# Attention decode with a mixer on one core: a filling unit's denominators and products at other steps, and V in loads of 16 cells ahead of a change of layer

## The chip, the cores and the metric

The kernel runs on one core of one Trainium2 chip. The metric is the device time of one execution in microseconds (us), as the median of several runs of the same program. The profile is of one further execution; its times count from the start of the span.

## What is computed

Two layers, each an attention block over a cached K and V and then a token mixer, for 2 batch rows of one token each:

```
x = x + A(layernorm(x)); x = x + B(layernorm(x)); x = x + A(layernorm(x)); x = x + B(layernorm(x))
A: q = x @ wq (32 heads of 128); scores = q.k * 128**-0.5 over 32768 cached positions;
   softmax; o = p @ v; result o @ wo.      8 heads of K and V, each for 4 heads of q
B: u = gelu(layernorm(x)^T w1 + b1), 1792 hidden; y = u w2 + b2
```

All data are float32. Both layers use the same weights and the same cache, so each layer reads the whole K and V of 2 x 8 head groups, and those reads are nearly all of the work: the arithmetic on them is small.

## The kernel before

**Units and cells.** A unit is (layer, batch row, K/V head): 2 x 2 x 8 = 32 units. A unit's K, and likewise its V, is 64 cells; a cell is a 128 x 512 float32 tile of 256 KB. One tile `mem` (line 220) holds 106 cells and takes everything that is loaded: K, V, and the weights of a head (8 cells).

**Steps.** `Order` (lines 41 to 110) writes out a list of 1024 steps by hand. A step works on 4 cells of one unit's K (`k_step`, line 328, the matmuls of line 335 into `scores`) or of its V (`v_step`, line 379, the matmuls of line 388 into `acc`); a phase of 16 steps is one unit's K or V. In the quiet parts K of a unit comes ahead of V of the unit before it. For a unit, between K and V: the maximum (`max_1`, `max_2`), the turned scores (line 365) and the exponentials on ScalarE (line 370), which leave partial sums in `lsum`. Behind V: `denominators` (line 407) adds the two sums on VectorE, sums over the partitions by a matmul (line 411) and takes the reciprocal (line 413); `take_out` (line 417) copies `acc` into a row tile; `out_1` (line 435) gathers the head's result by matmuls (line 427) and multiplies by the reciprocal (line 442); `out_2` (line 448) multiplies with `wo` into `rows` (line 451).

**The changes of layer.** Layer 1 of a batch row can start only when its layer 0 is done with attention and mixer. `Order` has two such changes, one for each batch row (`changes`, line 65): x is the last unit of the old layer, `fill` is a unit of the other batch row whose V phase runs while x's mixer is worked off, and y is the first unit of the new layer. The steps around the first change, with the numbers that the text uses: K of x (400 to 415), V of the last unit ahead of it, `before[-1]` (416 to 431), K of fill (432 to 447), V of x (448 to 463), V of fill (464 to 479), K of y (480 to 495), V of y (496 to 511). The second change has the same phases 96 steps later, with two K phases ahead of V of x. x and y share their K/V head, so the first 10 cells of K and all 64 of V that x loaded are kept in `mem` for y (`kept`).

**What hangs on which step.** `at(p, f, ...)` (line 707) makes a function run behind step p. For x, with e the last step of its V, the mixer is spread over the next steps: the layernorm at e + 2, the 14 Gelu tiles two by two with their projections from e + 3 to e + 10 (`hidden_tiles`, line 520), the copy of the rows (`take_rows`, line 463) at e + 10, and `change_0` to `change_3` (lines 565 to 594), which make y's query, at e + 11 to e + 14. For any unit whose V is not the last of its batch row and layer, `denominators` is at v_mid + 2 (two steps behind the middle of its V), `out_1` at v_end + 1 and `out_2` at v_end + 2 (lines 757 to 774). For fill, v0 = e + 1, so its denominators stood at e + 10.

**Loads and their planner.** `plan_loads` (line 113) decides, ahead of time, in which sizes and into which cells everything is loaded, and behind which step each load is issued. It goes through the steps with a clock of its own (line 34 on: 0.6024 us a cell, 1.6 us a step, and the `us` that `at` was given for the hooks), looks for each load at the sizes 32, 24, 16, 8 and 4 and at all places in `mem`, and takes the place that is free soonest. A load's step is the one behind which its cells were last read. `Order.sizes`, set by `cut` (line 97), fixes the size of chosen loads: K of y, V of fill in loads of 4 (line 93), the second half of V of x in 16, 8, 4, 4 (`TAPER`). All loads are issued by SP, in order, on one queue (line 823; weights line 816), each behind its step's semaphore and with at most 8 in flight; a load that waits holds up those behind it. The transfers of one queue are worked off in order by 16 DMA engines, each of which brings an equal part of each load.

Of the kernel before, what the change touches and what calls it, by code (L numbers as in the profile page):

```python
# [15 lines left out]
HALF = 32  # L16
# [24 lines left out]
class Order:  # L41


    def __init__(self, heads):
        far, f, s = list(range(heads - 2)), heads - 2, heads - 1
        self.steps = []
        self.pairs = []
        before = [(0, b, h) for h in far for b in (0, 1)] + [(0, 0, f)]
        x0, fill0, y0 = (0, 0, s), (0, 1, f), (1, 0, s)
        x1, fill1, y1, n = (0, 1, s), (1, 0, f), (1, 1, s), (1, 1, f)  # L50
        after = [(1, b, h) for h in far[:1:-1] for b in (0, 1)] + [(1, b, h) for b in (0, 1) for h in far[1::-1]]
        for i, u in enumerate(before):
# [12 lines left out]
        self.changes = ((x0, fill0, y0), (x1, fill1, y1))  # L65
        self.units = before + [x0, fill0, y0, x1, fill1, y1, n] + after
        self.first, self.end = {}, {}
        for p, (kind, u, g) in enumerate(self.steps):
            self.first.setdefault((kind, u), p)
            self.end[kind, u, g // HALF] = p  # L70
        byv = sorted(self.units, key=lambda u: self.first["V", u])
        self.v_before = {u: byv[i - 1] if i else None for i, u in enumerate(byv)}
        self.last_of = {
            (layer, b): max((u for u in self.units if u[:2] == (layer, b)), key=lambda u: self.end["V", u, 1])
            for layer in (0, 1)
            for b in (0, 1)
        }
        self.first_of = {
            (layer, b): min((u for u in self.units if u[:2] == (layer, b)), key=lambda u: self.end["V", u, 1])
            for layer in (0, 1)  # L80
            for b in (0, 1)
        }
        self.kept = {}
        for x, _, y in self.changes:
            for g in range(KEPT_K):
                self.kept["K", x, g] = ("K", y, g)
            for g in range(KEPT_V):
                self.kept["V", x, g] = ("V", y, g)
        self.sizes = {}
        for x, fill, y in self.changes:  # L90
            self.cut("K", y, KEPT_K, (-KEPT_K % STEP,) + (STEP,) * ((2 * HALF - KEPT_K) // STEP))
            self.cut("V", x, HALF, TAPER)
            self.cut("V", fill, 0, (STEP,) * 16)
        self.cut("V", self.last, 0, (HALF // 2, HALF // 2))
        self.cut("V", self.last, HALF, FINAL)
# [100 lines left out]
def gqa_mixer_kernel(ctx: ExitStack, tc: tile.TileContext, x, kt, v, wqo, cols, out):  # L196
# [10 lines left out]
    order = Order(HKV)  # L207
# [499 lines left out]
    def at(p, f, *args, us=0.0):  # L707
        hooks.setdefault(p, []).append((f, args))
        busy[p] = busy.get(p, 0.0) + us
# [6 lines left out]
    changed = {y: (x, fill) for x, fill, y in order.changes}  # L716
# [3 lines left out]
    for u in order.units:  # L720
# [6 lines left out]
        us = (u, mate) if b == 0 and mate not in made and (layer == 0 or h < HKV - 2) else (u,)  # L727
# [11 lines left out]
    for u in order.units:  # L739
        layer, b, h = u  # L740
        key = (layer, b)
        k_mid, k_end = end["K", u, 0], end["K", u, 1]
        v0, v_mid, v_end = first["V", u], end["V", u, 0], end["V", u, 1]
        ahead = order.v_before[u]
        p1, p2 = (k_end + 2, k_end + 4) if k_end + 4 < v0 else (k_end, k_end)
        t0 = max(k_mid, end["V", ahead, 0] if ahead else 0)
        t1 = max(k_end, end["V", ahead, 1] if ahead else 0)
        if p2 <= t0:
            at(p1, max_1, u, us=0.2), at(p2, max_2, u, us=0.2)
            at(t0, turn_scores, u, 0), at(t0, exponentials, u, 0)  # L750
        else:
            at(t0, turn_scores, u, 0)
            at(p1, max_1, u, us=0.2), at(p2, max_2, u, us=0.2)
            at(p2, exponentials, u, 0, us=5.0 if p1 == p2 else 0.0)
        at(t1, turn_scores, u, 1)
        at(max(t1, p2), exponentials, u, 1)
        at(v0 - 1 if u == order.last else v_mid + 2, denominators, u, us=0.4)
        if u == order.last:
            at(v0 - 1, take_rows, key)
            at(v0 - 1, table, AF.Gelu_apprx_tanh)  # L760
            at(v0 - 1, mix_1, key)
            at(v0 - 1, last_rows, u)
            at(v_mid, unread, u, G, 3)
            at(v_mid + 4, unread, u, P, 2)
            at(v_end - 2, take_out, u)
            at(v_end - 2, unread, u, G)
            at(v_end - 1, out_sum, u)
            at(v_end, last_mixer, u)
            continue
        at(v_end, take_out, u)  # L770
        if u != order.last_of[key]:
            late = 0 if u == order.v_before[order.last] else 1
            at(v_end + late, out_1, u, us=1.2)
            at(v_end + 2 * late, out_2, u, us=2.0)
            continue
        e = v_end
        at(e - 2, mix_1, key, us=1.2)
        at(e, out_1, u, us=1.9)
        at(e + 1, out_2, u, us=2.0)
        at(e + 1, take_rows, key)  # L780
        at(e + 2, mix_2, key, us=1.2)
        if layer == 0:
            at(e + 2, unread, u, G // 2)
            at(e + 3, half_way, key, us=1.0)
            at(e + 3, unread, u, G)
        at(e + 2, table, AF.Gelu_apprx_tanh)
# [103 lines left out]
```

## Time and profile before

| | us |
|---|---|
| median of 3 runs | 2505.46 (2503.72 to 2507.68) |
| the profiled execution | 2505.56 |
| its span, first to last instruction | 2503.7 |
| TensorE matmuls at work | 1380.4 |
| VectorE, ScalarE at work | 180.4, 185.9 |
| mean granted clock of TensorE | 0.756 of full speed |

The rows of the profile give a group of instructions or one of them: the line of the kernel, the engine (PE is TensorE, DVE VectorE, ACT ScalarE, POOL GpSimd, SP the engine that issues the loads), the operation, output and input tiles with shapes. In a timeline a row begins with start and duration in us and ends, in brackets, with the idle time of the engine ahead of it and what ended that. In the table of stretches the columns are each engine's busy time, then PEclk, the granted share of TensorE's clock, the busy share of the 16 DMA engines, and the rate in GB/s. A matmul of float32 stands as several records (8 for a step of 4 cells).

### The profile page before, as it was taken

How to read it: one execution, taken by the hardware profiler on the slowest of the kernel's cores; microseconds unless marked ns; L12 is line 12 of the kernel's file. 1: busy time of each engine (PE TensorE's matmuls, PEld its weight loads, DVE VectorE, ACT ScalarE, POOL GpSimd, SP SyncE). 2: the span in 40 equal slices, each digit the busy share in tenths (PEclk: the TensorE clock that was granted, in tenths of full speed). 3: DMA queues.
4: the chain of work that ended last, by engine and by line, in shares of the span. 5: the costliest groups of instructions: out<-in, count | busy, mean ns of one | idle time of the engine just before them, and what ended most of it. 6: DMA issues, size and time to landing. Idle time of an engine off the chain costs nothing. (4 is left out here: it accounts for less than half of the span.)

```text
span 2503.7 us, 21195 instructions
## 1 busy us (share of the span) xinstructions
PE 1380.4 (55%) x9682; PEld 395.1 (16%) x9682; DVE 180.4 (7%) x487; ACT 185.9 (7%) x579; POOL 5.2 (0%) x18
## 2 busy tenths in 40 slices
PE   3455555654555545556676773555554545555567
PEld 1111111111111111111121121111111111111112
DVE  1000000000000000001010010000000000000012
ACT  0100000000000000001110101000000000000021
POOL 0000000000000000000000000000000000000000
PEclk9777776777767776778887877777777777777788
DMA  9999999999999999999999999999999999999996
GB/s 418 431 425 436 434 431 434 434 430 432 432 434 432 430 433 434 416 430 418 407 426 427 417 424 438 432 433 429 434 434 430 434 435 428 430 436 432 432 428 278
DMA packets 33651, 1065.70 MB, mean 426 GB/s; under 512 B 3989, under 2 KB 3993, under 8 KB 5146
## 3 DMA queue, kind: packets, MB, share of 16 engines
q1 hardware_dynamic: 33272, 1064.32, 99.0%
q8 instruction: 76, 1.25, 0.2%
q14 instruction: 13, 0.11, 0.0%
q10 hardware_dynamic: 290, 0.03, 0.0%
HBM read 1064.33 MB, written 0.00 MB: 425 GB/s over the span
## 5 line engine op out<-in xcount | busy, mean ns | idle before, releaser
L388 PE MATMUL acc<-mem,S 128*16 128x512 f32 x4080 | 590.7, 711 | 575.5 <-DMA mem<-in_v_dram 570.6
L335 PE MATMUL scores<-mem,qz 128*32 128x512 f32 x4096 | 602.7, 729 | 516.8 <-DMA mem<-in_kt_dram 516.7
L370 ACT ACTIVATE S<-S,neg 128x128 f32<-128x128 f32 x256 | 129.7, 509 | 2240.4 <-DVE S L365 1201.3
L335 PEld LDWEIGHTS scores<-mem,qz 128*32 128x32 f32 x4096 | 135.9, 127 | 914.5 <-issue 470.4
L388 PEld LDWEIGHTS acc<-mem,S 128*16 128x16 f32 x4080 | 124.9, 106 | 890.1 <-issue 801.4
L345 DVE TENSOR_REDUCE mx<-scores 128x1 f32<-128x512 f32 x64 | 44.2, 691 | 803.9 <-PE scores L335 796.1
L427 PEld LDWEIGHTS misc<-selg,row 128*128 128x128 f32 x256 | 48.9, 285 | 48.2 <-issue 36.8
L427 PE MATMUL misc<-selg,row 128*128 128x4 f32 x256 | 51.7, 325 | 3.3 <-DVE row L419 3.3
L365 DVE STREAM_TRANSPOSE S<-scores 128x512 f32<-128x512 f32 x64 | 45.5, 710 | 111.6 <-PE acc L388 111.6
L451 PE MATMUL rows<-mem,oT 128*1 128x512 f32 x248 | 52.5, 936 | 0.3 <-DVE oT L442 0.3
L370 ACT ACTIVATION_READ_ACCUMULATOR S<-S,neg 128x1 f32 x256 | 47.7, 186 | 0.0
L355 DVE TENSOR_REDUCE m<-misc 1x4 f32<-1x128 f32 x32 | 8.9, 279 | 379.0 <-PE misc L353 379.0
L419 DVE COPY row<-acc 128x512 f32<-128x512 f32 x32 | 22.1, 692 | 176.1 <-PE acc L388 176.1
L413 DVE RECIPROCAL rl<-misc 128x4 f32<-128x4 f32 x32 | 5.8, 183 | 360.9 <-PE misc L411 360.9
L442 DVE TENSOR_TENSOR oT<-misc,rl 128x4 f32<-128x4 f32 x32 | 5.2, 162 | 273.1 <-PE misc L427 272.6
L411 PEld LDWEIGHTS misc<-both,one 128*128 128x128 f32 x64 | 14.4, 280 | 52.7 <-issue 46.8
L300 PE MATMUL misc<-mem,xw 128*32 128x512 f32 x144 | 20.0, 618 | 1.9 <-DVE xw L276 1.9
L353 PE MATMUL misc<-ident,mxa 128*1 128x128 f32 x64 | 18.5, 387 | 2.1 <-DVE mxa L351 2.1
L307 PEld LDWEIGHTS misc<-selg,row 128*128 128x128 f32 x128 | 16.3, 199 | 17.1 <-issue 8.6
L411 PE MATMUL misc<-both,one 128*128 128x4 f32 x64 | 17.1, 338 | 3.2 <-DVE both L410 3.2
L527 ACT ACTIVATE row<-bcast,bias,scale 128x512 f32<-128x512 f32 x21 | 16.3, 778 | 31.2 <-PE rows L511 14.2
L307 PE MATMUL misc<-selg,row 128*128 128x2 f32 (+1 forms) x128 | 17.7, 260 | 0.8 <-DVE row L292 0.8
(119 smaller groups left out, 245.6 us busy)
## 6 DMA issues: line engine op xcount, KB each, us to landing
mem<-in_kt_dram SPq DMA_DIRECT2D x20, 2048.0 KB, 16.1
mem<-in_v_dram SPq DMA_DIRECT2D x37, 1024.0 KB, 8.8
mem<-in_wqo_dram SPq DMA_DIRECT2D x14, 2048.0 KB, 32.0
mem<-in_kt_dram SPq DMA_DIRECT2D x28, 1024.0 KB, 9.1
mem<-in_v_dram SPq DMA_DIRECT2D x7, 4096.0 KB, 23.6
mem<-in_v_dram SPq DMA_DIRECT2D x4, 6144.0 KB, 26.3
mem<-in_kt_dram SPq DMA_DIRECT2D x6, 4096.0 KB, 23.8
mem<-in_v_dram SPq DMA_DIRECT2D x7, 2048.0 KB, 27.1
```

Source lines behind the costliest of these rows:

```text
L300: nc.tensor.matmul(q_ps[us][32 * d : 32 * d + 32, :], xw[:, d, :], wq[:, d, :], start=True, stop=True)
L307: nc.tensor.matmul(pt[:, r * n : (r + 1) * n], q_row[us][:, r * DH : (r + 1) * DH], side, start=True, stop=True,)
L335: nc.tensor.matmul(sc_ps[u, half][32 * row : 32 * row + 32, :], qz[:, at : at + 32], cells(at_cell["K", u, g], 1), start=(i == 0), stop=(i ...
L345: nc.vector.tensor_reduce(mx[u][:, half : half + 1], sc_ps[u, half], axis=AX.X, op=ALU.max)
L353: nc.tensor.matmul(pm[:1, :P], mxa, ident, start=True, stop=True)
L365: nc.vector.transpose(S[half], sc_ps[u, half])
L370: nc.scalar.activation(s[:, :, h], s[:, :, h], AF.Exp, bias=neg[u][:, h : h + 1], scale=SCALE, accum_out=lsum[u][:, half, h : h + 1],)
L388: nc.tensor.matmul(acc[32 * row : 32 * row + R * QT, :], S[half][:, col : col + R * QT], vc, start=(g < NG), stop=(g >= quads - NG),)
L411: nc.tensor.matmul(pl[:, :R], ones, both, start=True, stop=True)
L419: nc.vector.tensor_copy(asb[u], acc)
L427: nc.tensor.matmul(po_of[u][:, :R], asb[u][:, t * DH : (t + 1) * DH], selg[:, t * R : (t + 1) * R], start=(t == 0), stop=(t == QT - 1 and ...
L451: nc.tensor.matmul(rows[b][32 * r : 32 * r + 1, :], oT[u][:, r : r + 1], wo_of(u)[:, r, :], start=(u == order.first_of[layer, b]), stop=(u ...
```

## The change

Three edits. `Order` now also fixes V of the last unit ahead of the first change as four loads of 16 cells, and the first half of V of each x as two loads of 16. For the filling units, `denominators` moves from v_mid + 2 to v0 + 4, that is from e + 10 to e + 5, behind the third pair of Gelu tiles; and `out_1` and `out_2` move from v_end + 1 and v_end + 2 to v_end + 7 and v_end + 9, that is from behind y's first and second K steps to behind its seventh and ninth. The planner runs again on the new sizes and hook times, so the places and steps of other loads follow from it.

```
@@ class Order
         self.sizes = {}
+        self.cut("V", before[-1], 0, (HALF // 2,) * 4)
         for x, fill, y in self.changes:
+            self.cut("V", x, 0, (HALF // 2, HALF // 2))
             self.cut("K", y, KEPT_K, (-KEPT_K % STEP,) + (STEP,) * ((2 * HALF - KEPT_K) // STEP))
             self.cut("V", x, HALF, TAPER)
             self.cut("V", fill, 0, (STEP,) * 16)
@@ hooks of each unit
         at(t1, turn_scores, u, 1)
         at(max(t1, p2), exponentials, u, 1)
-        at(v0 - 1 if u == order.last else v_mid + 2, denominators, u, us=0.4)
+        fills = [y for y, (_, fill) in changed.items() if fill == u]
+        at(v0 - 1 if u == order.last else v0 + 4 if fills else v_mid + 2, denominators, u, us=0.4)
@@
         at(v_end, take_out, u)
         if u != order.last_of[key]:
-            late = 0 if u == order.v_before[order.last] else 1
+            late = 0 if u == order.v_before[order.last] else 7 if fills else 1
             at(v_end + late, out_1, u, us=1.2)
-            at(v_end + 2 * late, out_2, u, us=2.0)
+            at(v_end + (late + 2 if fills else 2 * late), out_2, u, us=2.0)
             continue
```

More of the change, by code (lines that the diff above doesn't have):

```diff
@@ L89, in __init__ @@
         self.sizes = {}
+        self.cut("V", before[-1], 0, (HALF // 2,) * 4)
         for x, fill, y in self.changes:
+            self.cut("V", x, 0, (HALF // 2, HALF // 2))
             self.cut("K", y, KEPT_K, (-KEPT_K % STEP,) + (STEP,) * ((2 * HALF - KEPT_K) // STEP))
@@ L756, in gqa_mixer_kernel @@
         at(max(t1, p2), exponentials, u, 1)
-        at(v0 - 1 if u == order.last else v_mid + 2, denominators, u, us=0.4)
+        fills = [y for y, (_, fill) in changed.items() if fill == u]
+        at(v0 - 1 if u == order.last else v0 + 4 if fills else v_mid + 2, denominators, u, us=0.4)
         if u == order.last:
@@ L771, in gqa_mixer_kernel @@
         if u != order.last_of[key]:
-            late = 0 if u == order.v_before[order.last] else 1
+            late = 0 if u == order.v_before[order.last] else 7 if fills else 1
             at(v_end + late, out_1, u, us=1.2)
-            at(v_end + 2 * late, out_2, u, us=2.0)
+            at(v_end + (late + 2 if fills else 2 * late), out_2, u, us=2.0)
             continue
```

## The prediction

> **What bounds the kernel now.** Three views, from coarse to fine. First the page: which engine is ever full?
>
> ```profile
> span 2503.7 us, 21195 instructions
> PE 1380.4 (55%) x9682; PEld 395.1 (16%) x9682; DVE 180.4 (7%) x487; ACT 185.9 (7%) x579; POOL 5.2 (0%) x18
> q1 hardware_dynamic: 33272, 1064.32, 99.0%
> q8 instruction: 76, 1.25, 0.2%
> L388 PE MATMUL acc<-mem,S 128*16 128x512 f32 x4080 | 590.7, 711 | 575.5 <-DMA mem<-in_v_dram 570.6
> L335 PE MATMUL scores<-mem,qz 128*32 128x512 f32 x4096 | 602.7, 729 | 516.8 <-DMA mem<-in_kt_dram 516.7
> ```
>
> No compute engine passes 55%, and nearly all the idle time of TensorE's two big lines ends on a DMA. Queue q1 is at work for 99% of the span. So the time is 1064.32 MB divided by the rate of the transfers, and a change that moves no bytes can win only what that rate loses somewhere. Second view: the rate by stretches, quiet ones first and last, the stretches around the two changes of layer between them.
>
> ```profile
> core 0: us, PE busy (x) PEld busy (x) DVE busy (x) ACT busy (x) POOL busy (x), PEclk, DMA share, GB/s
> 500.00:1000.00 500.00, 255.82 (x1736) 72.00 (x1732) 29.71 (x77) 25.32 (x96) 0.00 (x0) 0.72 1.00 432
> 1040.00:1100.00 60.00, 28.20 (x198) 7.13 (x198) 2.23 (x7) 2.11 (x8) 0.00 (x0) 0.72 0.98 415
> 1100.00:1150.00 50.00, 20.02 (x152) 5.99 (x144) 3.01 (x6) 2.11 (x8) 0.00 (x0) 0.70 0.97 418
> 1150.00:1230.00 80.00, 61.26 (x468) 19.56 (x472) 9.00 (x33) 17.95 (x35) 1.09 (x2) 0.93 1.01 423
> 1230.00:1270.00 40.00, 29.33 (x186) 5.54 (x182) 3.57 (x9) 4.14 (x16) 0.00 (x0) 0.71 1.00 402
> 1360.00:1435.00 75.00, 57.99 (x432) 16.86 (x428) 9.11 (x31) 15.88 (x27) 1.08 (x2) 0.90 1.01 419
> 1435.00:1475.00 40.00, 33.26 (x246) 9.02 (x242) 3.87 (x11) 4.14 (x16) 0.00 (x0) 0.79 0.99 412
> 1600.00:2400.00 800.00, 420.24 (x2868) 119.05 (x2870) 49.67 (x131) 47.09 (x167) 0.54 (x1) 0.73 1.00 432
> ```
>
> Quiet stretches run at 432 GB/s. Against that, a stretch loses its length times (1 - rate/432): 2.4 us in 1040-1100, 1.6 in 1100-1150, 1.7 in 1150-1230, 2.8 in 1230-1270, 2.3 in 1360-1435, 1.9 in 1435-1475. That is 12.7 us, half a per cent, and it is the ceiling. The two V stretches of the filling units (1150-1230 and 1360-1435) are transfers of 4 cells without a pause (share 1.01); the load lists that the planner's code gives for both kernels hold 65 loads of 4 cells each, so those 4.0 us stay. 8.7 us are left.
>
> Third view, the landings. A load counts as landed when the slowest of the 16 DMA engines has brought its part, and that is what TensorE waits for. Its own starts show it, in the K phase of the first new unit y:
>
> ```profile
> 1229.54 1.93 PE L335 MATMUL scores<-mem,qz 128*32 128x512 f32 x8 [1.43 <-DMA mem<-in_kt_dram]
> 1232.02 1.93 PE L335 MATMUL scores<-mem,qz 128*32 128x512 f32 x8 [0.55 <-DMA mem<-in_kt_dram]
> 1234.50 1.67 PE L335 MATMUL scores<-mem,qz 128*32 128x512 f32 x8 [0.55 <-DMA mem<-in_kt_dram]
> 1236.97 1.06 PE L335 MATMUL scores<-mem,qz 128*32 128x512 f32 x8 [0.80 <-DMA mem<-in_kt_dram]
> 1239.43 1.93 PE L335 MATMUL scores<-mem,qz 128*32 128x512 f32 x8 [1.40 <-DMA mem<-in_kt_dram]
> 1242.19 1.93 PE L335 MATMUL scores<-mem,qz 128*32 128x512 f32 x8 [0.83 <-DMA mem<-in_kt_dram]
> ...
> 1247.11 1.06 PE L335 MATMUL scores<-mem,qz 128*32 128x512 f32 x8 [0.75 <-DMA mem<-in_kt_dram]
> ```
>
> Each row is one step of 4 cells that starts as its load lands. The landings stand 2.46 to 2.48 us apart (the two gaps up to 1247.11 too); one gap, 1239.43 to 1242.19, is 2.76. So where the window says 2.8 us lost, the landings say 0.3. The same in the second change:
>
> ```profile
> 1439.75 1.93 PE L335 MATMUL scores<-mem,qz 128*32 128x512 f32 x8 [0.55 <-DMA mem<-in_kt_dram]
> 1442.69 1.93 PE L335 MATMUL scores<-mem,qz 128*32 128x512 f32 x8 [1.00 <-DMA mem<-in_kt_dram]
> ```
>
> One gap of 2.94, so 0.5 lost. The windows average over 16 engines, most of which were ahead and paused; the landings follow the slowest, and the end of the program waits for the slowest too. I weigh the landings more.
>
> **The change part by part.** The working starts from the profiled execution's 2505.56 us (span 2503.7 and 1.86 around it); the median of the runs, 2505.46, is 0.1 less.
>
> (a) V ahead of the first change in loads of 16. Before, V of the last unit ahead of the change came as 16+16+24+8 cells, K of the filling unit as 32+24+8, V of x as 24+8+16+8+4+4. After: 16+16+16+16, then 32+32, then 16+16+16+8+4+4. The first two loads wait for the same steps in both lists, so the thin place around 1060 stays. What follows differs (TensorE's timeline, with SP's row last):
>
> ```profile
> 1075.92 5.01 PE L388 MATMUL acc<-mem,S 128*16 128x512 f32 x32 [5.50 <-DMA mem<-in_v_dram]
> 1090.55 3.61 PE L388 MATMUL acc<-mem,S 128*16 128x512 f32 x16 [9.62 <-DMA mem<-in_v_dram]
> 1116.04 1.94 PE L335 MATMUL scores<-mem,qz 128*32 128x512 f32 x8 [15.51 <-DMA mem<-in_kt_dram]
> 1130.59 7.07 PE L335 MATMUL scores<-mem,qz 128*32 128x512 f32 x64 [2.13 <-DMA mem<-in_kt_dram]
> 1092.51 0.33 SPq L823 DMA_DIRECT2D mem<-in_kt_dram  x1
> ```
>
> Between 1090.55 and 1116.04 40 cells landed (8 of V, 32 of K), 10.49 MB, 24.3 us at 432 GB/s; it took 25.5. So at most 1.2 us are lost, at a load that SP could send only at 1092.51, since it waited for the step fed by the 24-cell load. After, the load of 16 and K's 32 both wait for step 423, the last of the four that start at 1075.92, so they go out near 1081, with 16 cells (9.7 us from 1075.9, to 1085.6) still on their way. No late load is left. From 1116.04 to 1130.59 24 cells took 14.55 us, the full rate, so nothing more is there to win. This part is worth between 0 and -1.2; a fetch of instructions (q8 is in the table above) can hold up one engine just as well, and I take a third, **-0.4**.
>
> (b) The list that follows. The planner places each load in the 106 cells by its own clock, so new sizes and due times shift all later places. For y's K, with steps counted from y's first, each load of 4 cells (named by its first cell) goes out behind this step:
>
> ```
> cell     24  28  32  36  40  44  48  52  56  60
> before    0   1   3   4   5   5   8   9  10  12
> after     1   3   4   5   7   7   8  10  10  12
> ```
>
> Both changes have these two rows. Before, SP sent nothing for 7.5 us (its timeline, then the time to landing of its loads from 1215 to 1245):
>
> ```profile
> 1225.68 0.80 SPq L823 DMA_DIRECT2D mem<-in_kt_dram  x2
> 1234.02 0.33 SPq L823 DMA_DIRECT2D mem<-in_kt_dram  x1
> 1244.19 1.28 SPq L823 DMA_DIRECT2D mem<-in_kt_dram  x3
> DMA to landing us min/median/max: 5.4/10.3/13.3
> ```
>
> The fastest load took 5.4 us from issue to landing, of which 2.5 are the transfer. So **a load is late on the slowest engine when less than 2.9 us of transfers are queued ahead of it**. Before, the load behind step 8 (1234.02) had three ahead, the last landing at 1239.4: 5.4 us, plenty. The one behind step 12 (1244.19) had two, the last landing at 1247.1: 2.9, just enough. After, step 7 starts at 1229.54 and is done 1.93 later; cells 40 and 44 go out at 1231.5 with cells 32 and 36 ahead, the last landing at 1234.5: 3.0. Step 10 starts at 1236.97 and is done 1.06 to 1.93 later, with two ahead to 1241.9 (2.48 behind 1239.43): 3.0 to 3.9. Step 12 again 2.9 to 3.9. So there are two or three thin places where there was one, all at the edge. Cost: if both pauses go with the old gaps, -0.8 by the landings and -4.7 by the windows; if each change pauses twice as often as it does now, +0.8 and +4.7. I stay near the landings' end and take **+0.5**. The Trainium skill ("DMA: Bandwidth & Descriptors", Anatomy of one DMA) puts the fixed part of a transfer at about 2.0 us, fitted on another issuing path; the 5.4 above leaves 2.9, so here the trace decides. By 2.0 every thin place has 0.9 to spare, +0.5 becomes 0, and the sum 2505.2.
>
> (c) The filling unit's denominators, from the last Gelu step to the third.
>
> ```profile
> 1201.04 0.69 DVE L465 COPY row<-rows 128x512 f32<-128x512 f32 x1 [15.46 <-PE rows L511]
> 1201.95 0.35 PE L411 MATMUL misc<-both,one 128*128 128x4 f32 x2 [1.04 <-DVE both L410]
> 1202.23 1.05 PE L388 MATMUL acc<-mem,S 128*16 128x512 f32 x8
> ```
>
> VectorE makes the sum `both` behind its copy of the rows, so TensorE's matmul stood 1.04 us for it, until 1201.95, and the V step behind it began 0.3 us late. Moved, the add and the reciprocal fall into VectorE's idle 15.46 us ahead of that copy, and the 0.35 of matmul among Gelu projections. TensorE's V steps here take 1.05 us (last row) and their loads of 4 cells land 2.5 us apart, so over a microsecond of each is free and covers 0.35 either way: between -0.3 and +0.4 per change by the rows, **0** taken, as no landing moves. If the cover went, it would be +0.7 for both changes.
>
> (d) The products, 7 and 9 steps behind V's end instead of 1 and 2.
>
> ```profile
> 1216.26 1.06 PE L427 MATMUL misc<-selg,row 128*128 128x4 f32 x8
> 1218.13 1.04 PE L451 MATMUL rows<-mem,oT 128*1 128x512 f32 x8
> 1222.22 1.07 PE L335 MATMUL scores<-mem,qz 128*32 128x512 f32 x8 [1.33 <-DMA mem<-in_kt_dram]
> ```
>
> 2.1 us of TensorE leave steps 0 to 3 of y's K, which run ahead of their data only until 1222.22. The 1.06 goes between steps 6 and 7, where TensorE stood 1.43 us (row 1229.54): hidden. The 1.04 goes behind step 8, whose own load is sent by then; the wait there is 0.55, so step 9 begins 0.5 late, but no load of the new list waits for step 9, and step 10 begins at its landing. VectorE's copy and product are early in both. Bounds: -2.1 to +2.1 per change, **0** taken. The Trainium skill ("TensorE: Matmul & The Clock Gate", Part 1) says that idling halves TensorE's clock and some microseconds of work restore it; the 1.93 and 1.06 for the same 8 matmuls agree. By it, products among these steps keep step 7 at 1.06, its loads leave 0.9 us sooner, +0.5 becomes 0, and the sum is again 2505.2.
>
> **Sum:** 2505.56 - 0.4 + 0.5 + 0 + 0 = **2505.7 us**. No DMA is added (230 loads for 231), none changes its queue, and bytes and the other instructions are the same in number.
>
> **Rivals.** *Faster, the pauses go:* the windows are right, not the landings. Then (b) gives -4.7 and (a) up to -1.6 (1100-1150): 2499.3. For it: 402 and 412 GB/s are real. Against it: the landings lost 0.8, and the new list keeps thin places. 5 in 100.
>
> *Slower, the ring runs dry:* two or three places at the edge become late loads, since step 7 and step 10 both run at the slow 1.93. It decides when queued work falls under 2.9 us, so from a TensorE delay of 0.1 us at step 7. Price: the pauses' windows again for each of them, 4.7 for a second one, up to 9.4 for a third; with (a) not gained, 2510.3 to 2515.0, 2511 as its value. For it: 3.0 against 2.9. Against it: before had 2.9 at 1244.19, and the next landings, to 1247.1, were not late. 10 in 100.
>
> *Slower by the products:* TensorE gets behind at steps 7 and 9 for want of cover, 2.1 us in each change straight into landings: +4.2, 2509.8, still within 0.2%. 4 in 100.
>
> *Nothing moves:* the cuts shift loads that nobody waits for, 2505.6. This can't be told from the forecast and shares its chance, 81 in 100.
>
> **How the numbers follow.** 0.2% is 5.0 us, about what a measurement of this kernel can tell from no change. Faster by more: the first rival, 0.05. Slower by more: the second, about 0.09 of its 0.10. Within: 0.86. The single terms' far ends are -6.3 and +9.4; they hold each other off, so the forecast's own range is 2503 to 2508.5, and with half of the two larger rivals 2501.5 to 2510.5.
>
> **What would show it.** In the changed kernel's trace: (a) SP sends two loads near 1081 and none near 1092, and 25.5 us becomes about 24.3; (b) loads of y's K leave at about 1231.5, 1234 and 1238, and gaps of landings stay under 2.9 us; more than two gaps above 3 per change mean the second rival; (c) no wait of L411 on VectorE at 1201; (d) L427 just ahead of 1229.5 and L451 near 1234, with L335's waits on DMA between them. Wrong I am if 1230-1270 and 1435-1475 come to 425 GB/s or more (the first rival) or fall under 385.

## The result, and the profile after

The changed kernel takes **2508.44 us** (median of 20 runs, 2505.84 to 2516.12) beside 2505.38 for the kernel before on the same chip (20 runs, 2502.66 to 2510.19). The ratio is 1.0015, with a 95% interval of 1.0008 to 1.0021: 3.1 us or 0.15% slower, small but clear of zero. The forecast was 2505.7, its range 2501.5 to 2510.5. So the direction and the bounds held, and the size of the loss did not: 3.1 measured, 0.1 to 0.2 forecast (2505.7 beside the profiled execution's 2505.56 and the median of 2505.46). The direction owes something to luck: it was what was left of two close estimates, -0.4 and +0.5.

The first view is the page of the changed kernel. The lines are those shown of the kernel before, two line numbers higher in the code (L337 is K's matmul, L390 V's).

```profile
span 2507.4 us, 21193 instructions
PE 1396.2 (56%) x9682; PEld 398.8 (16%) x9682; DVE 180.5 (7%) x487; ACT 185.8 (7%) x579; POOL 5.2 (0%) x18
q1 hardware_dynamic: 33128, 1064.32, 98.9%
L390 PE MATMUL acc<-mem,S 128*16 128x512 f32 x4080 | 596.7, 719 | 553.8 <-DMA mem<-in_v_dram 548.9
L337 PE MATMUL scores<-mem,qz 128*32 128x512 f32 x4096 | 609.9, 738 | 527.8 <-DMA mem<-in_kt_dram 527.4
```

The same bytes, the same number of matmuls, TensorE still idle for its loads. The page cannot say where 3 us went; the table of stretches can, at least roughly.

```profile
core 0: us, PE busy (x) PEld busy (x) DVE busy (x) ACT busy (x) POOL busy (x), PEclk, DMA share, GB/s
1040.00:1100.00 60.00, 30.69 (x190) 7.39 (x194) 2.23 (x7) 2.11 (x8) 0.00 (x0) 0.70 0.98 413
1100.00:1150.00 50.00, 27.80 (x196) 7.95 (x184) 3.46 (x8) 2.11 (x8) 0.00 (x0) 0.75 0.99 425
1150.00:1230.00 80.00, 57.90 (x428) 17.37 (x428) 8.57 (x31) 17.98 (x35) 1.09 (x2) 0.90 1.01 420
1230.00:1270.00 40.00, 28.74 (x202) 6.27 (x202) 3.57 (x9) 4.14 (x16) 0.00 (x0) 0.77 0.99 400
1360.00:1435.00 75.00, 57.92 (x432) 18.09 (x424) 9.12 (x31) 15.88 (x27) 1.08 (x2) 0.91 1.00 411
1435.00:1475.00 40.00, 31.04 (x226) 8.55 (x230) 3.87 (x11) 4.14 (x16) 0.00 (x0) 0.78 0.97 402
```

1100-1150 rose from 418 to 425 GB/s. The second change fell: 1360-1435 from 419 to 411, 1435-1475 from 412 to 402. TensorE's timeline of y's K in the second change shows the places. A row with x8 is one step of 4 cells, x16 two; the last row is y's first V.

```profile
1416.53 1.06 PE L337 MATMUL scores<-mem,qz 128*32 128x512 f32 x8 [1.41 <-DMA mem<-in_kt_dram]
1419.01 1.93 PE L337 MATMUL scores<-mem,qz 128*32 128x512 f32 x8 [1.42 <-DMA mem<-in_kt_dram]
1420.87 1.87 PE L429 MATMUL misc<-selg,row 128*128 128x4 f32 x8
1422.67 3.39 PE L337 MATMUL scores<-mem,qz 128*32 128x512 f32 x16
1425.89 1.03 PE L453 MATMUL rows<-mem,oT 128*1 128x512 f32 x8
1426.75 1.03 PE L337 MATMUL scores<-mem,qz 128*32 128x512 f32 x8
1430.12 1.07 PE L337 MATMUL scores<-mem,qz 128*32 128x512 f32 x8 [2.34 <-DMA mem<-in_kt_dram]
...
1440.70 1.07 PE L337 MATMUL scores<-mem,qz 128*32 128x512 f32 x8 [1.07 <-DMA mem<-in_kt_dram]
1444.96 1.94 PE L337 MATMUL scores<-mem,qz 128*32 128x512 f32 x8 [3.19 <-DMA mem<-in_kt_dram]
...
1451.84 2.76 PE L390 MATMUL acc<-mem,S 128*16 128x512 f32 x12 [2.40 <-ACT S L372]
```

Count the steps from the end: 1444.96 is step 15, 1430.12 step 10, 1416.53 step 5. Two steps stand far behind their forerunners, step 10 by 3.37 us and step 15 by 4.26, and both wait for a DMA. From the start of step 5 to that of step 15 are ten loads of 4 cells, 24.8 us at their undisturbed distance of 2.48. Here it took 28.43; before it took 25.27 (1417.42 to 1442.69). This one number, **step 5 to step 15**, is the measure of most experiments below, since it looks only at the place and not at what a run lost earlier.

Why is step 10's load late? It, with step 11's, was sent here (SP's timeline; first the changed kernel, then the kernel before):

```profile
1424.67 0.91 SPq L826 DMA_DIRECT2D mem<-in_kt_dram  x2
```

```profile
1418.55 0.81 SPq L823 DMA_DIRECT2D mem<-in_kt_dram  x2
```

Six microseconds later, and behind step 7 instead of step 5, as the table in the prediction said. In the trace the last load ahead of it landed at 1426.37: 1.7 us of transfers were left in the queue, and the new load landed at 1430.07, 5.4 us after it was sent. (A load has landed when the last of the 16 DMA engines has brought its part; the trace has the time of each part, and times of landing that stand in no row are from there.)

Step 15's load was sent here:

```profile
1437.38 0.33 SPq L826 DMA_DIRECT2D mem<-in_kt_dram  x1
```

The load ahead of it landed at 1440.66, so 3.3 us were queued, more than the 2.9 that the prediction asked for. It still landed 4.26 us behind that one, at 1444.92.

### The profile page after: what moved, and what is told of

Its sections match the earlier page's. It is cut to its first block, busy times and chain, and to the rows that moved or that the text cites. A ratio compares the mean times of both kernels' runs of the same rounds, so it can differ in the third digit from the quotient of the medians.

```text
span 2507.4 us, 21193 instructions
## 1 busy us (share of the span) xinstructions
PE 1396.2 (56%) x9682; PEld 398.8 (16%) x9682; DVE 180.5 (7%) x487; ACT 185.8 (7%) x579; POOL 5.2 (0%) x18
## 5 line engine op out<-in xcount | busy, mean ns | idle before, releaser
L390 PE MATMUL acc<-mem,S 128*16 128x512 f32 x4080 | 596.7, 719 | 553.8 <-DMA mem<-in_v_dram 548.9
L337 PE MATMUL scores<-mem,qz 128*32 128x512 f32 x4096 | 609.9, 738 | 527.8 <-DMA mem<-in_kt_dram 527.4
L337 PEld LDWEIGHTS scores<-mem,qz 128*32 128x32 f32 x4096 | 138.0, 129 | 933.3 <-issue 487.4
L390 PEld LDWEIGHTS acc<-mem,S 128*16 128x16 f32 x4080 | 125.8, 107 | 876.1 <-issue 775.0
L429 PEld LDWEIGHTS misc<-selg,row 128*128 128x128 f32 x256 | 49.7, 289 | 48.9 <-issue 39.3
L429 PE MATMUL misc<-selg,row 128*128 128x4 f32 x256 | 52.5, 328 | 3.3 <-DVE row L421 3.3
L413 PEld LDWEIGHTS misc<-both,one 128*128 128x128 f32 x64 | 13.5, 264 | 50.3 <-issue 45.7
L413 PE MATMUL misc<-both,one 128*128 128x4 f32 x64 | 16.4, 326 | 2.0 <-DVE both L412 2.0
```

The lines of the kernel that those rows point to most:

```text
L337: nc.tensor.matmul(sc_ps[u, half][32 * row : 32 * row + 32, :], qz[:, at : at + 32], cells(at_cell["K", u, g], 1), start=(i == 0), stop=(i ...
L390: nc.tensor.matmul(acc[32 * row : 32 * row + R * QT, :], S[half][:, col : col + R * QT], vc, start=(g < NG), stop=(g >= quads - NG),)
L413: nc.tensor.matmul(pl[:, :R], ones, both, start=True, stop=True)
L429: nc.tensor.matmul(po_of[u][:, :R], asb[u][:, t * DH : (t + 1) * DH], selg[:, t * R : (t + 1) * R], start=(t == 0), stop=(t == QT - 1 and ...
```

## The experiments

Each was timed in five rounds against the kernel before on the same chip. Beside them the kernel before took 2505.66 us (runs 1 to 4), 2505.45 (5 to 8), 2505.48 (9 to 11) and 2506.73 (12). The theory at the start: the loss comes from y's K loads, which the new list sends later. The rivals: the loads of 16, the denominators, or the products holding TensorE at steps 7 and 9.

**1. The change without the late products** (edit against the changed kernel):

```
-            late = 0 if u == order.v_before[order.last] else 7 if fills else 1
+            late = 0 if u == order.v_before[order.last] else 1
-            at(v_end + (late + 2 if fills else 2 * late), out_2, u, us=2.0)
+            at(v_end + 2 * late, out_2, u, us=2.0)
```

> The changed kernel with the products back behind y's first and second K steps; the V loads of 16 and the early denominators stay. The planner then gives y's K the old list (nothing behind step 7). Theory 1, the new list of y's K loads costs the 3 us: they are gone, about 2505.0, since the late load of 1092 is gone too. Theory 2, the products themselves cost by holding TensorE at steps 7 and 9: the same, 2505.0. Theory 3, the loads of 16 ahead of the first change cost: 2508.4 stays. V of the second y begins about 1449 by theories 1 and 2, about 1452 by theory 3 (1449.6 before, 1451.8 in the changed kernel).

Measured: 2504.61, ratio 0.9998 (0.9989 to 1.0006). Steps 5 to 15 took 24.83 us in the first change and 24.81 in the second. The loss is gone, with the loads of 16 and the early denominators still in. What also went: without the late products the planner gives y's K the places in `mem` that it had before.

**2. The late products alone** (the kernel before with the last edit of the change and nothing else).

> The kernel before with only the products moved to 7 and 9 steps behind V's end. The planner gives y's K a list that sends two loads behind step 7, as in the changed kernel. Theories 1 and 2: about 3 to 3.5 us over before, 2508.5 to 2509, with a gap of landings of over 3 us behind step 9 of the second y. Theory 3: no difference from before, 2505.4.

Measured: 2515.38, ratio 1.0036 (1.0022 to 1.0049; 5 runs). The planner made a third list, of 239 loads. For the ten loads of y's K from cell 24 on, its first change has the steps and places of the changed kernel's list; its second has the same steps from cell 40 on, and six other places. Steps 5 to 15 took 27.03 and 25.79 us, 2.5 more than before in all (25.04 and 25.27), and the stretch 1230-1270 fell to 388 GB/s. That is half of the 5.2 us by which this profiled execution (2510.87) was slower, and a quarter of the median's 9.7; the rest lies elsewhere in that list and stays open.

**3. The whole change with the old list**: the products run late, but the planner is told of them at the old steps.

```
-    def at(p, f, *args, us=0.0):
+    def at(p, f, *args, us=0.0, plan=None):
-        busy[p] = busy.get(p, 0.0) + us
+        plan = p if plan is None else plan
+        busy[plan] = busy.get(plan, 0.0) + us
...
+            late_1, late_2 = (7, 9) if fills else (late, 2 * late)
+            plan_1, plan_2 = (1, 2) if fills else (late, 2 * late)
+            at(v_end + late_1, out_1, u, us=1.2, plan=v_end + plan_1)
+            at(v_end + late_2, out_2, u, us=2.0, plan=v_end + plan_2)
```

> All of the change in what the engines do, products at 7 and 9 included, but the planner is told that the products are at 1 and 2, so that y's K keeps the old list. Theory 1 (the list): 2505.0. Theory 2 (the products hold TensorE): step 7 still begins late, but no load hangs on it in this list, and the load behind step 8 has 5 us queued: 2505.0 to 2506. Theory 3 (loads of 16): 2508.4. A result near 2508 with a late step 7 would say that the products cost by another way than the loads.

Measured: 2504.44, ratio 0.9996 (0.9987 to 1.0005); steps 5 to 15 in 24.84 and 24.82 us. In its second change TensorE was held by the products just as in the changed kernel:

```profile
1421.13 1.87 PE L429 MATMUL misc<-selg,row 128*128 128x4 f32 x8
1422.93 3.41 PE L337 MATMUL scores<-mem,qz 128*32 128x512 f32 x16
1426.16 1.03 PE L453 MATMUL rows<-mem,oT 128*1 128x512 f32 x8
1427.02 1.03 PE L337 MATMUL scores<-mem,qz 128*32 128x512 f32 x8
1429.18 1.06 PE L337 MATMUL scores<-mem,qz 128*32 128x512 f32 x8 [1.13 <-DMA mem<-in_kt_dram]
```

Step 10 begins at 1429.18, on the beat, because its load had been sent earlier. So with this list the late products cost nothing that shows in the time. The list decides.

**4. The new list alone**: as in 3, but `late_1, late_2 = (1, 2)` and `plan_1, plan_2 = (7, 9)`.

> The other cross: the planner is told that the products are at 7 and 9 and gives the changed kernel's list of loads to the letter, but the products run behind y's first and second K steps as before. Theory 1 (the list alone): 2508.4, the loads behind step 7 are late with no help of the products. Theory 2 (the products): step 7 begins as its data land and its loads leave about 1.2 us sooner in the second change, with 3 us queued: 2505.0 to 2506, and no gap of landings over 3 us at y's cells 40 to 43.

Measured: 2507.49, ratio 1.0008 (0.9999 to 1.0017): by the interval just short of clear. The profile is plainer: 26.84 and 27.11 us from step 5 to step 15, and in the second change this gap, with TensorE free of the products (TensorE's rows of steps 8 to 10):

```profile
1425.53 1.67 PE L337 MATMUL scores<-mem,qz 128*32 128x512 f32 x8 [0.56 <-DMA mem<-in_kt_dram]
1427.97 1.06 PE L337 MATMUL scores<-mem,qz 128*32 128x512 f32 x8 [0.76 <-DMA mem<-in_kt_dram]
1432.27 1.93 PE L337 MATMUL scores<-mem,qz 128*32 128x512 f32 x8 [3.24 <-DMA mem<-in_kt_dram]
```

Step 10's load, with step 11's, is this row of SP's timeline:

```profile
1425.03 0.81 SPq L829 DMA_DIRECT2D mem<-in_kt_dram  x2
```

The load left at 1425.03, with transfers queued until step 9's landing at 1427.97: 2.9 us, which the prediction called just enough. The next landing came 4.30 later, not 2.48.

**5. The denominators alone** (the kernel before with the second edit of the change).

> The kernel before with only the denominators moved among the Gelu tiles; every load is the same, behind the same step. Theory 1 (the list of y's K loads costs): no difference, 2505.5 within 1 us, since landings set the pace there and TensorE had over a microsecond of idle time a step. A rival: the earlier denominators free TensorE ahead of y's query and win about 1 us, which would be what the kernels with the old list show.

Measured: 2504.92, ratio 0.9998 (0.9989 to 1.0007); 24.79 us in both changes. Nothing to see, as forecast.

**6. The changed kernel's list with the products at steps 6 and 9** (`late_1, late_2 = (6, 9)`, `plan_1, plan_2 = (7, 9)`), so that they no longer stand ahead of step 7.

> The changed kernel with its list of loads to the letter, but the first products one step earlier, 6 steps behind V's end, ahead of a step that no load waits for. Step 7 then begins as its data land, also where the clock is low. Theory 1 (the list alone): about 2507.5, as with the list and early products, since 2.9 us of queued transfers are too few by themselves. Theory 2 (the products hold step 7): about 2505.5. The changed kernel itself has 2508.4.

Measured: 2508.99, ratio 1.0015 (1.0006 to 1.0023), no better than the change. Its profiled execution, though, was the fastest of the eleven, at 2505.36 us: 24.83 and 26.39 us. With the new list the loss differs from one execution to the next.

**7. Two loads put behind a later step** (the kernel before; the steps of cells 40 and 44 overwritten in the finished list, their places left):

```
+    held = {("K", y, g) for y in changed for g in (40, 44)}
+    loads = [(l, n, c, first["K", l[1]] + 7 if l in held else p) for l, n, c, p in loads]
```

> The kernel before with one thing changed: of y's K, the loads of cells 40 and 44 are held back from step 5 to step 7, in both changes of layer; places, sizes, order and all hooks stay. Theory 1: this alone brings most of the loss, 2 to 3 us over before, 2507.5 to 2508.5, with a gap of landings of over 3 us ahead of cells 40 in one or both changes. If it does not (under 1 us over before), the list costs by its other places: the steps of cells 24, 28 and 52, or the loads behind y's V.

Measured: 2505.53, ratio 0.9997 (0.9988 to 1.0006); 24.83 and 25.38 us. At first this looked like the end of the theory. Run 9 showed what it was worth.

**8. A try at something faster**: run 1 with the second half of K of x in two loads of 16 as well.

```
+            self.cut("K", x, HALF, (HALF // 2, HALF // 2))
```

> A version to beat both: loads of 16 and early denominators as in the change, products back behind y's first and second K steps (the old list of y's K loads), and also the second half of K of x in two loads of 16 instead of one of 32, so that V of the last unit ahead of the change need not wait until 1062 for its second load. If the pause there costs its full window (about 2 to 3 us): 2502 to 2503. If, as the landings say, it costs little because the slowest engine never paused: 2504 to 2504.5, like the kernel without the late products.

Measured: 2505.18, ratio 1.0003 (0.9994 to 1.0012). The stretch 1040-1100 stayed at 416 GB/s (415 before). No gain.

**9, 10, 11. Whole rows put behind later steps.** In the kernel before, the steps in the list were overwritten for all of y's K (run 9), for its cells 24 to 36 (run 10), and for the K that follows it (run 11). Run 9:

```
+    row = {24: 1, 28: 3, 32: 4, 36: 5, 40: 7, 44: 7, 52: 10}
+    held = {("K", y, g): first["K", y] + k for y in changed for g, k in row.items()}
+    loads = [(l, n, c, held.get(l, p)) for l, n, c, p in loads]
```

> The kernel before, with the same loads in the same cells, and with all of y's K held to the new list's steps: the loads of cells 24, 28, 32 and 36 go out behind steps 1, 3, 4 and 5 (before: 0, 1, 3 and 4), those of cells 40 and 44 behind step 7, that of cell 52 behind step 10. Nothing else of the change is in it. Theory (the steps of y's K in the new list cost the time): from 2505.5 to about 2508.5, 1230-1270 at 395 GB/s or less, 1435-1475 at 410 or less, a landing gap of more than 3.5 us in the second change. Rival (the row is covered by what is queued, and the loss comes with other cells and with the K loads that follow): 2505 to 2506, both windows at 415 or more.

> The kernel before, with only the loads of y's cells 24, 28, 32 and 36 held one step later (behind steps 1, 3, 4 and 5), so that one load of 1 MB fewer is in flight in steps 0 to 5. If the queue's depth there is what the new list costs: 2507 to 2508.5, with 1230-1270 or 1435-1475 under 410. If the depth there is more than enough: 2505 to 2506. If it is only both together with the two loads behind step 7 (held alone they cost nothing), this stays at 2505.5 and the kernel with the whole row goes up.

> The kernel before, with y's K as it was and only the loads behind it held as in the new list: in the first change the next unit's K from cell 22 on goes out behind steps 499, 500, 504 and 510 (before: 497, 497, 501 and 507), in the second one load behind step 594 (before: 593). Theory (y's own row costs the time): 2505.5, no difference. Rival (the loads that follow y's K cost it): 2507.5 to 2508.5, with 1270-1360 or 1475-1600 lower by 5 GB/s or more.

Measured: 2503.74 (0.9999, 0.9990 to 1.0008), 2503.26 (0.9994, 0.9985 to 1.0003) and 2505.40 (1.0004, 0.9995 to 1.0013): no difference in any. But the edits had not done what they were written for. In run 9 step 10's load should have waited for step 7. SP's row of it, then TensorE's rows of steps 5 to 7:

```profile
1417.05 0.80 SPq L826 DMA_DIRECT2D mem<-in_kt_dram  x2
```

```profile
1415.92 1.07 PE L335 MATMUL scores<-mem,qz 128*32 128x512 f32 x8 [1.28 <-DMA mem<-in_kt_dram]
1418.41 1.94 PE L335 MATMUL scores<-mem,qz 128*32 128x512 f32 x8 [1.42 <-DMA mem<-in_kt_dram]
1420.89 1.93 PE L335 MATMUL scores<-mem,qz 128*32 128x512 f32 x8 [0.55 <-DMA mem<-in_kt_dram]
```

It left at 1417.05, as step 5 ended (1415.92 + 1.07), and before step 7 had begun. The section on the kernel before says that each load goes out behind its step's semaphore; these runs show it more exactly. A step in the list only sets a load's place in the program; SP runs ahead, and what a load truly waits for is the last reader of the cells that it overwrites (this one goes into 94 to 97, which steps 4 and 5 read). Run 7's left at 1416.37 in the same way, and in all four runs the loads that were to be held left as the same steps ended as in the kernel before. So runs 7, 9, 10 and 11 said nothing on the theory, for or against. They show instead that the *places* have to be changed, and, as they move their loads at the same steps as the kernel before, how far such kernels scatter: ratios of 0.9994 to 1.0004.

**12. The new places alone.** The kernel before, same sizes, same order, products early; only y's K goes to the places of the new list, in both changes (cell of K above, cell of `mem` below):

```
cell of y's K   24   28   32   36   40   44   48   52   56   60
before          24   28  102   98   94   90  102   98   94  102
after           28  102   98   94  102   90   98  102   94   98
```

```
+    cell = {24: (28, 1), 28: (102, 3), 32: (98, 4), 36: (94, 5), 40: (102, 7)}
+    cell.update({44: (90, 7), 48: (98, 8), 52: (102, 10), 56: (94, 10), 60: (98, 12)})
+    moved = {("K", y, g): (c, first["K", y] + k) for y in changed for g, (c, k) in cell.items()}
+    moved["K", (0, 1, 7), 10] = (94, 495)
+    loads = [(l, n, *moved.get(l, (c, p))) for l, n, c, p in loads]
```

The new row leaves cells 24 to 27 of `mem` empty, so the places behind them move up by one. Seven of the ten loads then wait for a reader one or two steps further on, those of cells 40 and 44 for step 7 instead of step 5; the loads of cells 48, 56 and 60 wait for the same step as before.

> The kernel before, with the same loads, sizes and order, the products early and no V loads of 16; only the cells of SBUF into which the last ten loads of y's K go are those of the new list in both changes (28, 102, 98, 94, 102, 90, 98, 102, 94, 98 in place of 24, 28, 102, 98, 94, 90, 102, 98, 94, 102), and in the first change one K load behind them goes one step later, because it shares cells with y's last one. This is asked because in the kernels whose loads were only put behind later steps (the two loads, the first four, the whole row, the next K) SP sent them at the same times as before (cells 40 and 44 of the second change 1417.05 us in the kernel with the whole row, 1418.55 in the kernel before): what times a load is the last reader of the cells that it goes into, and those kernels left the cells alone. Theory (the new cells are read later, so the loads leave later and the queue runs thin): cells 40 and 44 of the second change leave SP about 1424 to 1425, as in the changed kernel and in the one with only its list, one or two landing gaps over 3.5 us in a change, second V of y at 1450 or later, time 2507 to 2509. Rival (what costs is in the rest of the list): loads leave later but land without a gap, 2505 to 2506.

Measured: steps 5 to 15 took 25.58 and **28.32 us** (28.43 in the changed kernel). SP's rows of step 10's and step 13's loads, then TensorE's rows of steps 9 to 13:

```profile
1423.82 0.80 SPq L828 DMA_DIRECT2D mem<-in_kt_dram  x2
1432.46 0.80 SPq L828 DMA_DIRECT2D mem<-in_kt_dram  x2
```

```profile
1427.07 1.06 PE L335 MATMUL scores<-mem,qz 128*32 128x512 f32 x8 [1.14 <-DMA mem<-in_kt_dram]
1430.47 1.94 PE L335 MATMUL scores<-mem,qz 128*32 128x512 f32 x8 [2.34 <-DMA mem<-in_kt_dram]
1432.95 1.94 PE L335 MATMUL scores<-mem,qz 128*32 128x512 f32 x8 [0.54 <-DMA mem<-in_kt_dram]
1435.41 1.93 PE L335 MATMUL scores<-mem,qz 128*32 128x512 f32 x8 [0.53 <-DMA mem<-in_kt_dram]
1439.89 1.93 PE L335 MATMUL scores<-mem,qz 128*32 128x512 f32 x8 [2.55 <-DMA mem<-in_kt_dram]
```

The loads left when the theory said (1423.82 for "about 1424 to 1425"), and the gaps came: 3.40 at step 10, 4.48 at step 13. The time was 2507.55, ratio 1.0005 (0.9996 to 1.0015): inside the 2507 to 2509 expected, but only 0.8 us over its own kernel before (2506.73), and the interval takes in the change's 1.0015 as well as no loss. So the time does not settle whether y's places make up all of the loss. It is the profile that carries this run, together with the table of all of them (one profiled execution each):

| y's K in | kernel | steps 5 to 15, first + second change, us | median us |
|---|---|---|---|
| old places | before | 25.04 + 25.27 | 2505.38 |
| | 1, 3, 5, 8 | 24.83 + 24.81, 24.84 + 24.82, 24.79 + 24.79, 24.84 + 24.84 | 2504.61, 2504.44, 2504.92, 2505.18 |
| | 7, 9, 10, 11 | 24.83 + 25.38, 25.93 + 25.01, 24.83 + 24.81, 24.84 + 24.83 | 2505.53, 2503.74, 2503.26, 2505.40 |
| later places | change | 26.21 + 28.43 | 2508.44 |
| | 2, 4, 6, 12 | 27.03 + 25.79, 26.84 + 27.11, 24.83 + 26.39, 25.58 + 28.32 | 2515.38, 2507.49, 2508.99, 2507.55 |

The sums of the old places lie between 49.58 and 50.94, mean 49.93; those of the later places between 51.22 and 54.64, mean 53.31. No kernel crosses over, in the profile or in the ratio of times (0.9994 to 1.0004 and 1.0005 to 1.0036), though the two ratios at the border lie close together. The difference of the means is **3.4 us**.

Does the depth of the queue make the late loads, as the theory says? For each of the ten loads of y's K from cell 24 on, in both changes of all 14 kernels, the traces give how much was queued when it was sent (until the landing of the load ahead) and how far its landing came behind that one, beyond 2.48 us (one profiled execution each; the border of 4.0 us was drawn with the numbers at hand):

| y's K in | queued, us | loads | over 0.5 us late | late in all, us |
|---|---|---|---|---|
| old places | 4.0 or more | 162 | 1 | 1.3 |
| | under 4.0 | 18 | 1 | 1.6 |
| later places | 4.0 or more | 74 | 0 | 2.6 |
| | under 4.0 | 26 | 11 | 16.0 |

So it does: 16.0 of the 18.6 us that the five kernels with the later places lost come with their 26 thinly covered loads, two or three in each change; the old places have one in each change. Also at like depth the later places were late more often (11 of 26 beside 1 of 18), and why is not shown.

No version beat the kernel before: the lowest of those that keep the change's other edits, run 3 at 2504.44, has an interval that takes in no difference.

## Why the prediction was right, and where it was not

**(a) V in loads of 16: -0.4, about right, for another reason.** The two loads were to leave near 1081 with none at 1092 (SP's timeline, the changed kernel):

```profile
1082.04 0.33 SPq L826 DMA_DIRECT2D mem<-in_v_dram  x1
1082.41 0.42 SPq L826 DMA_DIRECT2D mem<-in_kt_dram  x1
```

They did, and SP sent nothing more until 1102.15. V's last 16 cells start at 1095.57 and K's first step at 1114.93:

```profile
1095.57 6.50 PE L390 MATMUL acc<-mem,S 128*16 128x512 f32 x32 [3.26 <-DMA mem<-in_v_dram]
1114.93 1.94 PE L337 MATMUL scores<-mem,qz 128*32 128x512 f32 x8 [12.85 <-DMA mem<-in_kt_dram]
```

The 32 cells between them took 19.36 us, where 432 GB/s gives 19.42: no loss is left there. But the load sent late, at 1092.51, had not lost anything before either. In the kernel before, its 32 cells landed 19.38 us behind V's last 8 (1096.62 to 1116.00). Those 8 cells, sent at 1070.19, are what came late: 6.21 us behind the load ahead, where 432 GB/s gives 4.85. Fifteen engines had brought their part by 1095.29, the last at 1096.62; a fetch of instructions of 1.04 us began at 1094.07. That fits the fetch which the prediction named beside its own cause; which engine the fetch was on, the trace does not tell.

Over all kernels the size came out. From the landing of V's second load of 16 cells to that of K's first load (64 cells, 38.8 us at 432 GB/s) the eight kernels with the old loads there took 38.8 to 40.8 us, mean 39.5 (the kernel before 40.1), and the six with loads of 16 took 39.0 to 39.4, mean 39.2. That is 0.3 less, within the scatter. The times can't show it: of the runs that keep this part and not the new places, 1 and 3 have ratios of 0.9998 and 0.9996, and 8 has 1.0003, none clear of 1.

**(b) y's K loads: the step that failed.** The sign was right, and so was the table of steps behind which the loads go out. The loads of cells 40, 48 and 52 left at 1230.21, 1232.70 and 1236.94 in the first change, each 1.1 to 1.3 us ahead of the forecast since the whole phase had begun earlier. The thin places were there, and the gaps did not stay under 2.9 us, as the forecast had it; but there were at most two over 3 us in a change, so by the prediction's own test it was not yet the rival in which the ring runs dry. What was wrong is the price: +0.5 forecast, **+3.4** by the measure above. In the medians, beside their own kernel before, the change stands 3.1 us higher and runs 4, 6 and 12 stand 1.8, 3.5 and 0.8.

The price rested on a threshold: a load is late when under 2.9 us are queued ahead, and places at 2.9 to 3.9 cost next to nothing. The runs bear out neither half. The 5.4 us at 1244.19, from which it was taken, do not measure what a load needs: 2.9 us were queued ahead of that load and its transfer takes 2.48, so it could not land sooner. In the first change of run 6, step 10's load left with 2.5 us queued (the load ahead landed at 1233.13) and was on the beat all the same; it landed at 1235.62, 2.49 us behind. SP's row, then TensorE's row of step 10:

```profile
1230.63 0.80 SPq L829 DMA_DIRECT2D mem<-in_kt_dram  x2
```

```profile
1235.66 1.06 PE L337 MATMUL scores<-mem,qz 128*32 128x512 f32 x8 [1.32 <-DMA mem<-in_kt_dram]
```

And places on the safe side were late: 2.9 us queued cost 1.8 us in run 4 (4.30 for 2.48) and 2.0 in run 12 (4.48); 3.9 and 3.3 cost 1.1 and 1.8 in the two changes of the changed kernel. At 1.7 queued the loss was 1.2 there, just 2.9 less 1.7, but 1.5 and 0.6 in run 2. So a place under 4 us is a draw, between nothing and 2 us. By the table of depths the later places have some five of them in a kernel, late by 0.6 us on average: about 3 us.

The Trainium skill ("DMA: Bandwidth & Descriptors", Anatomy of one DMA) gives a fixed part of about 2.0 us, for another issuing path. The trace agrees for most of the engines in one thinly covered load: of that sent at 1424.67, fifteen of the 16 had brought their part 4.2 to 4.5 us later, which is 1.7 to 2.0 more than the 2.48 of the transfer. The last one took 5.4, and it is the last one that TensorE waits for.

The prediction also named a wrong cause for the new list. It put it down to new sizes and due times together. Run 1 has the new sizes and the old row; run 3 differs from the changed kernel, and run 1 from run 4, only in the steps at which the products' 1.2 and 2.0 us are booked with the planner, and the loss goes with the booking. The edit that costs is thus the third one, not by its matmuls but by what it tells `plan_loads`.

**(c) The denominators: 0, held.** Run 5 shows no difference. In the changed kernel no L413 is left at the copy of the rows near 1201, and V's next step waits for its load alone:

```profile
1201.25 0.69 DVE L467 COPY row<-rows 128x512 f32<-128x512 f32 x1 [11.99 <-PE rows L513]
1202.10 1.05 PE L390 MATMUL acc<-mem,S 128*16 128x512 f32 x8 [0.99 <-DMA mem<-in_v_dram]
```

**(d) The products: 0, held for the whole, not for the place.** In the first change they lie as forecast:

```profile
1225.73 1.07 PE L337 MATMUL scores<-mem,qz 128*32 128x512 f32 x8 [1.41 <-DMA mem<-in_kt_dram]
1226.72 1.05 PE L429 MATMUL misc<-selg,row 128*128 128x4 f32 x8
1228.22 1.93 PE L337 MATMUL scores<-mem,qz 128*32 128x512 f32 x8 [0.44 <-DMA mem<-in_kt_dram]
1230.71 1.94 PE L337 MATMUL scores<-mem,qz 128*32 128x512 f32 x8 [0.56 <-DMA mem<-in_kt_dram]
1232.42 1.93 PE L453 MATMUL rows<-mem,oT 128*1 128x512 f32 x8
```

Step 7 at 1228.22 still waits 0.44 us for its load, so `out_1` is hidden. In the second change it was not: step 6 fell into a slow spell (1.93, not 1.07), L429 took 1.87 for 1.05, and step 7 began at 1422.67 with no wait, 1.2 us after its load had landed (1421.46 in the trace). That made step 10's load 1.2 us later and its queue 1.7 instead of 2.9 us. So "hidden in 1.43 us of idle time" counted a cost at one clock and a cover at another. Run 3 shows what this costs where the places are good, nothing; runs 4 and 6 show the loss without it.

The Trainium skill ("TensorE: Matmul & The Clock Gate", Part 1) ties the slow spells to idling. From it the prediction made that products among these steps would keep step 7 at 1.06. The rows above give 1.93, with L429 directly ahead and 0.44 us idle between, so that conclusion was wrong. It does not contradict the Trainium skill, which asks there for some microseconds of work: step 6 and L429 together worked from 1225.73 to 1227.77, 2.0 us.

**The rivals.** "Faster, the pauses go" fell: 402 and 400 GB/s in 1230-1270 of the two kernels, while run 1 raised that stretch to 424 and 1435-1475 to 414 and yet stayed at 2504.61, far from 2499.3. Landings, not windows, were the right scale for gains. "The ring runs dry" had the right mechanism, a queue that gets thin, at a price between the forecast's and its own; its condition, the same 2.9 us, was as wrong as the forecast's. "Slower by the products" fell with run 3.

## What to carry to other kernels

When a planner of transfers is told of work at other times, compare the places that it picks, not only the sizes and the order: a load leaves when the last reader of the memory under it is done, and four cells left empty put seven of the ten loads behind them one or two steps back. Price a queue that runs down to the edge as a chance at each place, not as a threshold with one lucky example on the safe side; and take a load's time to landing as a measure of its fixed cost only if nothing was queued ahead of it. And before an experiment that holds something back is read, look in its trace whether it was held at all.

## What was not expected of the hardware

With the same 2.9 us of transfers queued, a load of 1 MB came 2.48, 4.30 and 4.48 us after the one ahead of it. The lateness belongs to a few of the 16 engines. In run 12 the first engine had its part of step 13's load at 1436.85 and half of them by 1437.24, but the slowest at 1439.85. Of step 15's load in the changed kernel thirteen engines had their part 4.2 to 4.6 us after it was sent, the other three after 5.7, 6.1 and 7.5. In the loads of run 12's phase ahead of step 13 the first and the last engine were 1.4 to 2.0 us apart.

A thin queue is not the only way to a late load: in the first change of the kernel before, step 4's load was sent with 5.1 us queued and landed 4.15 us behind the one ahead, the last engine 1.7 us after the fifteenth, with a fetch of instructions of about 1 us at 1220.01. This lies just ahead of the steps that the measure covers. For thin places fetches alone do not explain it: one falls near 1424 in kernels with the gap (1424.14 in the changed kernel) and without it (1423.75 before), and none falls on step 13 of run 12. Why a thin queue sometimes leaves one engine so far behind was not settled.
